# A bucketed attention with a bilinear MLP behind it, on one core: the first two chunks' products by weight group, late weight conversions, bfloat16 scale products and a new order

## The chip, the core and the metric

The kernel runs on one core of a Trainium2 chip. TensorE is written PE, its weight load PEld, VectorE DVE, ScalarE ACT, GpSimd POOL, and SyncE, which here issues all DMAs, SP. The metric is the time of one execution on the device in microseconds (us); lower is better.

## What is computed

Four batches of eight heads, 768 positions, 64 values each. Queries and keys get a bucket of six signs from a projection; a query attends only to keys of its own bucket. The heads' outputs, side by side, are the rows x of a bilinear MLP.

```python
mask = q_bucket[:, :, :, None] == k_bucket[:, :, None, :]
scores = np.where(mask, scale * np.matmul(q, k.transpose(0, 1, 3, 2)), -1000000000.0)
scores = scores - np.max(scores, axis=-1, keepdims=True)
attn = np.exp(scores)
attn = attn / (np.sum(attn, axis=-1, keepdims=True) + 1e-09)
x = np.matmul(attn, v)            # (4, 8, 768, 64), then (3072, 512)
out = ((x @ w_a) * (x @ w_b)) @ w_out      # 512 -> 1536 -> 512
```

## The kernel before

All products run on 16-bit numbers in two parts: each operand is scaled by a power of two and split into a high part and a remainder (`hi`, `lo`), and three of the four partial products are added in PSUM.

**Chunks and query tiles.** The 3072 rows are 12 chunks of 256 (four batches, `NCH` = 3 chunks each). A chunk has two halves of four heads, and each half eight *query tiles* of 128 queries of one head: 192 in all. A query tile (`qtile`, L984) is a chain over all engines. PE makes 128 x 768 scores in PSUM (L1004, four products, tile `s`); DVE takes their maximum `mx` (L1016) and the width (L1025); ACT or DVE makes the bias, ACT the exponentials `e` with their sum (L1048); DVE, ACT or POOL casts them to 16 bits (L1056 to L1058) and POOL or DVE subtracts the cast to get the remainder (L1068, L1072), both into `a2`; SP issues a DMA that turns `a2` into `at` (L1078); PE multiplies it by V (L1087, 18 products, `av`). There are two PSUM tiles `s`, three tiles `e`, four `a2` and three `at`.

**The MLP of a chunk** (`moe`, L1261) has 12 blocks of 128 of the 1536 columns. For each, PE makes a and b (L1285, 24 products into `ab`), ACT copies a with its scale (L1299), DVE multiplies (L1307, `g`), ACT or DVE casts g, POOL subtracts (L1327), and PE adds the block's part of the output (L1337, six products into `o`). Chunk 0 closes `o` after every four blocks, since each of the three groups of weights has a scale of its own (`per_q`, `whole`); the other chunks close it once, with one scale for all (`one_scale`).

**Weights.** w_a and w_b come in three groups of 512 columns each, w_out in three groups of 512 rows: nine conversions (`w_group`, `wo_group`). A group's 64-bit words (`words`, L519) land in four staging tiles or in the places of w_out; DVE takes maxima (L617), PE spreads them over partitions by two fp32 passes with `ident` (L572), a chain of one-column operations on DVE makes the scales, ACT works on the words in place (L540, L548), DVE joins them to fp32 (L555), ACT casts and POOL subtracts (`hi_lo`, L633, L638). K, Q and V of each batch are scaled in the same way (`scale_of`, L450 to L470), K for each pair of heads, and K and Q are turned, so that d lies on partitions, together with their bucket marks in one tile `marked` (`turn`, `buckets`). In batch 0 all four K pairs and the first Q are turned by PE (L834) and copied out of PSUM (L842, L844); all others by DMA (L823).

**What sets the order.** Every operation is recorded with a number, and the table `ORDER` lists the numbers in the order in which they are issued; each engine runs its own in that order. A number of 10000 or more takes another engine for the operation; a negative one issues that many filler products of PE into the unused `ab` (`fill`, L1439, tile `warm`). The keys in the constants (`K0`, `V0`, `WG0`, `MF0` ...) only document where the table comes from; no order is computed from them here.

## Time and profile before

| | |
|---|---|
| median of 3 runs | 922.95 us (919.64 to 923.08) |
| span of the profiled execution, first to last instruction | 918.4 us |
| PE busy | 864.2 us, 94% |
| DVE, ACT, POOL busy | 681.2 us (74%), 543.9 us (59%), 433.0 us (47%) |
| granted PE clock, mean | 0.996 of 2.4 GHz |
| moved by DMA | 147.4 MB in 435950 packets |

The profiled execution's own time is its span and what lies around it: the runs lie 1.2 to 4.7 us above the span. Busy shares are means over a start, in which tiles are prepared and weights converted, and a long stretch in which chunks follow each other; so the windows (busy time of each engine in a stretch) say more than the page's first line. PE's busy time is modelled from pipelined products, so a price of a product is better read as the distance between two starts.

### The profile page before, as it was taken

To read this page: it belongs to the slowest core of one execution; us is meant where nothing else is said; L and a number is where in the kernel's file an instruction comes from. 1 tells how busy PE (TensorE), PEld (TensorE's weight loads), DVE (VectorE), ACT (ScalarE), POOL (GpSimd) and SP (SyncE) were. 2 spreads that over 40 slices of the span, in tenths; PEclk is the share of its full clock that TensorE was granted. 3 is DMA by queue.
4 is the path that set the end of the run, shared out by engine and by line. 5 is a ranking of instruction groups with operands and counts; after the bars stand their busy time and mean duration, and the time that the engine had idled before them with its cause. 6 is when DMAs were issued, how large, how long until landed. Compare 5 with 4: busy or idle time off the path is not lost.

```text
span 918.4 us, 23592 instructions
## 1 busy us (share of the span) xinstructions
PE 864.2 (94%) x9429; PEld 658.4 (72%) x9429; DVE 681.2 (74%) x1622; ACT 543.9 (59%) x1034; POOL 433.0 (47%) x372
## 2 busy tenths in 40 slices
PE   5667789999999999999999999999999999999998
...
DVE  7999999998988778777976757776888863752311
...
GB/s 330 222 238 235 191 224 229 163 189 194 175 193 184 144 144 197 185 172 153 176 110 187 107 141 163 151 208 151 154 187 169 156 126 113 130 111 70 1 24 24
DMA packets 435950, 147.40 MB, mean 161 GB/s; under 512 B 407552, under 2 KB 428160, under 8 KB 435840
## 3 DMA queue, kind: packets, MB, share of 16 engines
...
## 4 chain that ended last, share of the span: by engine, by line
PE 73%; DVE 9%; ACT 1%; issue 1%; DMA 1%; SPq 0%; ACTq 0%; DVEq 0%
PE ab L1285 36%; PE o L1337 18%; PE s L1004 10%; PE av L1087 8%; DVE mx L1016 2%; DVE xz L1187 1%; DVE g L1307 1%; DMA at<-a 1%; SPq L823 0%; PE b_k L795 0%; PE b_q L795 0%; DVE x L1126 0%; DVE width L1025 0%; DVE vl L781 0%; PE ps_v L450 0%
## 5 line engine op out<-in xcount | busy, mean ns | idle before, releaser
L1285 PE MATMUL ab<-xT,wab 128*128 128x256 f16 x3456 | 408.2, 273 | 3.0 <-DVE g L1307 1.8
L1285 PEld LDWEIGHTS <-wab 128*128 128x128 f16 x3456 | 333.1, 98 | 56.3 <-issue 4.1
L1068 POOL TENSOR_TENSOR a<-e,a 128x768 f16<-128x768 f32 x137 | 230.5, 1686 | 132.6 <-ACT a L1057 71.8
L1048 ACT ACTIVATE e<-s,bias,width 128x768 f32<-128x768 f32 x192 | 189.9, 989 | 83.2 <-DVE bias L1038 67.2
L1327 POOL TENSOR_TENSOR g<-g,g 128x256 f16<-128x256 f32 x144 | 106.2, 738 | 235.0 <-ACT g L1315 144.0
L1337 PE MATMUL o<-wo,g 128*128 128x512 f16 x864 | 209.3, 379 | 0.4 <-DVE ob L1373 0.4
L1016 DVE TENSOR_REDUCE mx<-s 128x1 f32<-128x768 f32 x192 | 181.6, 949 | 26.6 <-PE s L1004 25.8
L1307 DVE SCALAR_TENSOR_TENSOR g<-ab,wlow,a 128x256 f32<-128x256 f32 x132 | 63.6, 482 | 139.8 <-ACT a L1299 127.4
L1299 ACT ACTIVATE a<-ab,wlow 128x256 f32<-128x256 f32 x132 | 62.1, 471 | 162.8 <-PE ab L1285 161.4
L1087 PEld LDWEIGHTS <-at 128*128 128x128 f16 x3456 | 123.0, 98 | 25.3 <-DMA at<-a 5.6
L1337 PEld LDWEIGHTS <-g 128*128 128x128 f16 x864 | 81.9, 98 | 74.8 <-issue 0.6
L1087 PE MATMUL av<-vh,at 128*128 128x64 f16 x2304 | 126.4, 193 | 5.2 <-DMA at<-a 3.8
L1004 PE MATMUL s<-kTA_k,qTA_q 128*128 128x384 f16 x384 | 93.7, 326 | 18.2 <-ACT e L1048 13.9
L1004 PE MATMUL s<-kTB_k,qTB_q 128*128 128x384 f16 x384 | 93.7, 326 | 0.0
L1058 POOL CAST a<-e 128x768 f16<-128x768 f32 x57 | 51.1, 896 | 64.6 <-ACT e L1048 56.4
L1057 ACT CAST a<-e 128x768 f16<-128x768 f32 x92 | 76.0, 830 | 1.9 <-DMA at<-a 0.4
L1087 PE MATMUL av<-vl,at 128*128 128x64 f16 x1152 | 65.2, 193 | 0.0
L1315 ACT CAST g<-g 128x256 f16<-128x256 f32 x99 | 39.7, 401 | 38.2 <-DVE g L1307 33.0
L1004 PEld LDWEIGHTS <-qTA_q 128*128 128x128 f16 x384 | 34.7, 98 | 38.2 <-issue 20.8
L1032 ACT ACTIVATE bias<-mx,width 128x1 f32<-128x1 f32 x91 | 26.4, 292 | 57.1 <-DVE width L1025 56.9
L1072 DVE TENSOR_TENSOR a<-e,a 128x768 f16<-128x768 f32 x55 | 55.0, 1000 | 4.3 <-ACT a L1057 3.9
L1004 PEld LDWEIGHTS <-qTB_q 128*128 128x128 f16 x384 | 37.5, 98 | 24.9
...
## 6 DMA issues: line engine op xcount, KB each, us to landing
...
at<-a SPq DMA_TRANSPOSE x192, 4.1
```

What stands on the lines that cost most here:

```text
L1004: nc.tensor.matmul(ps.t[:, jj, :HALF], lhsT=x.t[:, uq, :], rhs=y.t[:, h * NT + jj * 3 : h * NT + jj * 3 + 3, :].rearrange("p t x -> p (t x)"),
L1016: lambda: nc.vector.tensor_reduce(out=mx.t[:, u : u + 1], in_=halves(ps.t), axis=AX.XY, op=ALU.max, negate=True),
L1048: lambda: nc.scalar.activation(flat2(e.t), halves(ps.t), AF.Exp, bias=bias.t[:, u : u + 1], scale=width.t[:, u : u + 1], accum_out=sm.t[:, ...
L1057: ("ACT", 0.725, lambda: nc.scalar.copy(out=a2.t[:, 0], in_=e.t), False),
L1068: lambda: nc.gpsimd.tensor_tensor(out=a2.t[:, 1], in0=e.t, in1=a2.t[:, 0], op=ALU.subtract),
L1072: lambda: nc.vector.tensor_tensor(out=a2.t[:, 1], in0=e.t, in1=a2.t[:, 0], op=ALU.subtract), True,
L1087: nc.tensor.matmul(av.t[:, u, :], lhsT=at.t[:, a + kt, :], rhs=w.t[:, h, kt, :], start=i == 0, stop=i == 3 * NT - 1,)
L1285: nc.tensor.matmul(pl.t[:, m, :CH], lhsT=wt(m, wi, cc, f), rhs=xt.t[:, :, xi * NC + cc, :], start=i == 0, stop=i == 3 * NC - 1,)
L1299: lambda a=a, pl=pl, gr=gr: nc.scalar.activation(a.t, pl.t[:, 0, :CH], AF.Copy, scale=cuts[:, gr : gr + 1]),
L1307: lambda a=a, g32=g32, pl=pl, gr=gr: nc.vector.scalar_tensor_tensor(out=g32.t, in0=pl.t[:, 1, :CH], scalar=cuts[:, gr + 1 : gr + 2], in1=a ...
L1327: lambda g=g, g32=g32: nc.gpsimd.tensor_tensor(out=g[1].t, in0=g32.t, in1=g[0].t, op=ALU.subtract),
L1337: nc.tensor.matmul(po.t[:, u, :], lhsT=g[gi].t[:, us], rhs=wo[f // 2].t[:, f % 2, wi * DM : (wi + 1) * DM], start=f % per_q == 0 and i == ...
```

## The change

The change has five parts.

- **Products by weight group in two chunks.** `SPLIT` = 2: chunks 0 and 1 run their blocks in the order group 0 of chunk 0, group 0 of chunk 1, group 1 of chunk 0, and so on, and close `o` after each group; chunk 1 closes it three times where it closed once.
- **Conversions later.** Only group 0 is converted ahead of its use; groups 1 and 2 are loaded and converted between the products of the groups before them. In group 0 and 1, w_a and w_b share one chain of scales.
- **Words in free slots.** The staging tiles `stg`, `W1`, `W2` (later w_out's places), still unused slots of `wab` and `raw` tiles take the words. Some conversions work on half a tile.
- **Scales by bfloat16 products.** `spread` multiplies the upper 16 bits of a maximum by a bfloat16 identity: one pass in place of two. Batch 0 has one chain for the scales of all four V pairs.
- **A new order**, without fillers, in which K pairs 1 to 3 of batch 0 are turned by DMA (`K_BY_PE` = 1).

```diff
-NE, NA, NAT, NRAW = 3, 4, 3, 2
-POOL_CASTS, POOL_EVERY = 20.26, 4
+NE, NA, NAT, NRAW = 3, 4, 3, 3
+K_BY_PE = 1
+SPLIT = 2
+POOL_CASTS, POOL_EVERY = 0, 4
 ORDER = [
-    12, 6, 5, 52, 0, 2, 1, 40, 3, 13, 60, 4, 296, 53, 14, 295, 7, 299, 15, -1, 8, 16, 300, 10017, 273, 41, 19, 277, 9,
...
+    HOMES = [
+        [("W1", "W2"), (20, 16), ("stg", 10)], [(18, "W2"), ("W1", "stg"), ("W2", 18)],
+        [("W2", "stg"), ("W2", "stg"), ("stg", "raw")],
+    ]
+    def spread(mx, cols, out):
+        for i, c in enumerate(cols):
+            nc.tensor.matmul(
+                out[:, i * P : (i + 1) * P],
+                lhsT=mx.t[:, c : c + 1].bitcast(BF16)[:, 1:2].to_broadcast([P, P]), rhs=identb, start=True, stop=True,
+            )
+    def largest(out, ps, n):
+        nc.vector.tensor_reduce(
+            out=out, in_=ps[:, : n * P].rearrange("p (n x) -> p n x", n=n), axis=AX.X, op=ALU.max
+        )
...
-            lambda: nc.tensor.matmul(
-                ps.t[:, 0, :P], lhsT=mx.t[:, 0:1].to_broadcast([P, P]), rhs=ident, start=True, stop=True
-            ),
+        op("PE", 0.06 * n, lambda: spread(mx, range(n), flat()), key, r=["identb", *((mx, i) for i in range(n))], w=[ps])
...
+    def words(src, home, name, key):
+        if home == "raw":
+            pieces = [buf("raw", [P, WP, 2], I32, f"raw_{name}{i}", NRAW) for i in range(2)]
+        elif isinstance(home, int):
+            pieces = [Slots(home, f"raw_{name}")]
+        else:
+            pieces = [buf(home, [P, 2 * WP, 2], I32, f"raw_{name}", 1, cp)]
...
-    HOME_K0 = [("wo0", 1, cp), ("wo1", 1, cp), ("raw", NRAW, p2), ("raw", NRAW, p2)]
-    HOME_V0 = [("a2", NA, p2)] * 2 + [("at", NAT, p2)] * 2
+    HOME_K0 = [("W0", 1, cp), ("e", NE, p2), ("e", NE, p2), ("e", NE, p2)]
+    HOME_V0 = [("a2", NA, p2)] * 4
...
-        turn(B, 2 * NT, tB, key, [(B, "hi"), (B, "lo")], n, None if b else TURN[0])
+        pe = b == 0 and hp < K_BY_PE
+        turn(B, 2 * NT, tB, key, [(B, "hi"), (B, "lo")], n, TURN[0] if pe else None)
...
-        whole = b or c
+        whole = b * NCH + c >= SPLIT
-        for f in range(NF):
+        for f in range(fqs[0] * (WP // P), (fqs[-1] + 1) * (WP // P)):
...
-                for g in range(NG):
-                    w_group(g, WG0[g], WC0[2 * g : 2 * g + 2], WH0[2 * g : 2 * g + 2])
                 for fq in range(NFQ):
-                    wo_group(fq, WO0[fq], OC0[2 * fq : 2 * fq + 2], OH0[2 * fq : 2 * fq + 2])
+                    for ms in ([0, 1],) if fq < 2 else ([0], [1]):
+                        w_groups(fq, ms, WG0[fq], WC0[fq], WH0[fq])
+                    wo_group(fq, WO0[fq], [OC0[fq]] * 2, [OH0[fq]] * 2)
...
+                elif m == SPLIT - 1:
+                    for fq in range(NFQ):
+                        for x in range(SPLIT):
+                            moe(b, x, [fq], [MF0[SPLIT * fq + x]] * NFQ, pace, lag, False)
```

Three places show what the new order moves. The first is DVE at the first query tiles. Before, behind the fourth score maximum (a row `mx` names batch, chunk and half; the `s` it reads ends with pair, head and tile):

```order
L1016 TENSOR_REDUCE mx_0_0_0_422<-s_0_0_0_0_1_1_538 128x1
L883 SCALAR_TENSOR_TENSOR nB_k0_3_516<-rk_k0_3_83,ks_k0_3_555,nB_k0_3_516 128x12x64
L617 TENSOR_REDUCE wmx_w3_503<-raw_w3_1_424 128x1
L1025 TENSOR_SCALAR width_0_0_0_457<-mx_0_0_0_422,qsig_q0_0_454 128x1
L1038 TENSOR_SCALAR bias_0_0_0_463<-mx_0_0_0_422,width_0_0_0_457 128x1
L973 TENSOR_SCALAR qsig_q0_0_454<-kinv_70,qmx_q0_0_152 128x1 x2
L626 TENSOR_REDUCE wmx_w3_503<-wmx_w3_503 128x1
L617 TENSOR_REDUCE wmx_wo0_511<-raw_wo0_0_206 128x1
L617 TENSOR_REDUCE wmx_wo0_511<-raw_wo0_1_507 128x1 x2
L578 TENSOR_REDUCE al_w3_695<-ps_w3_668 128x1
L626 TENSOR_REDUCE wmx_wo0_511<-wmx_wo0_511 128x1
```

And in the change, from the same maximum to the next two:

```order
L1077 TENSOR_REDUCE mx_0_0_0_377<-s_0_0_0_0_1_1_432 128x1
L1086 TENSOR_SCALAR width_0_0_0_399<-mx_0_0_0_377,qsig_q0_0_296 128x1
L1013 TENSOR_SCALAR qmx_q0_1_440<-qmx_q0_1_440 128x1
L1016 TENSOR_SCALAR qmx_q0_1_440<-qmx_q0_1_440 128x1
L1020 RECIPROCAL qsc_q0_1_453<-qmx_q0_1_440 128x1
L659 TENSOR_REDUCE wmx_w0ab_243<-raw_w0ab_0_0_268 128x1
L659 TENSOR_REDUCE wmx_w0ab_243<-wab_78 128x1
L1077 TENSOR_REDUCE mx_0_0_0_377<-s_0_0_0_1_0_0_466 128x1
L1077 TENSOR_REDUCE mx_0_0_0_377<-s_0_0_0_1_0_1_471 128x1
```

Before, 28 rows stand between the fourth maximum and the fifth, most of them scales and weight rows; now six do.

The second place is SP's queue at the first turns of attention (`at`). Before:

```order
L1078 DMA_TRANSPOSE at_0_0_0_0_0_532<-a_0_0_0_0_0_0_505 128x12x128
L1078 DMA_TRANSPOSE at_0_0_0_0_1_575<-a_0_0_0_0_0_1_529 128x12x128
L927 DMA rq_q_1_84<-in_q_dram 128x8x128
L519 DMA raw_w_0_585<-in_moe_w_a_dram 128x1024 x2
L519 DMA raw_w_1_626<-in_moe_w_a_dram 128x1024 x2
L1078 DMA_TRANSPOSE at_0_0_0_1_0_693<-a_0_0_0_0_1_0_610 128x12x128
L1078 DMA_TRANSPOSE at_0_0_0_1_1_746<-a_0_0_0_0_1_1_691 128x12x128
L823 DMA_TRANSPOSE qTB_q_1_820<-nB_q_1_711 128x16x128
L519 DMA raw_w_1_882<-in_moe_w_b_dram 128x1024 x2
L519 DMA raw_w_0_922<-in_moe_w_b_dram 128x1024 x2
```

In the change:

```order
L883 DMA_TRANSPOSE kTB_k_1_329<-nB_k_1_165 128x12x128
L563 DMA wab<-in_moe_w_b_dram 128x1024
L563 DMA raw_wo_0_0_360<-in_moe_w_out_dram 128x1024
L988 DMA rq_q_1_90<-in_q_dram 128x8x128
L883 DMA_TRANSPOSE kTB_k_2_402<-nB_k_2_350 128x12x128
L883 DMA_TRANSPOSE kTA_k_1_428<-marked 128x12x128
L1139 DMA_TRANSPOSE at_0_0_0_0_0_443<-a_0_0_0_0_0_0_416 128x12x128
L769 DMA rk_k_3_88<-in_k_dram 128x2x384
L563 DMA raw_wo_0_0_360<-in_moe_w_out_dram 128x1024
L1139 DMA_TRANSPOSE at_0_0_0_0_1_461<-a_0_0_0_0_0_1_425 128x12x128
L1139 DMA_TRANSPOSE at_0_0_0_1_0_478<-a_0_0_0_0_1_0_458 128x12x128
```

Turns of K now stand between the loads and the turns of attention, and fewer weight loads do.

The third is POOL, whose remainders `g1` carry batch, chunk and block in their names. Before, at blocks 6 to 9 of chunk 0:

```order
L1327 TENSOR_TENSOR g1_0_0_6_2708<-g_0_0_6_2594,g0_0_0_6_2603 128x256
L638 TENSOR_TENSOR wo4_2735<-wo_y4_2648,wo4_2735 128x2x512
L1327 TENSOR_TENSOR g1_0_0_7_2791<-g_0_0_7_2743,g0_0_0_7_2748 128x256
L1068 TENSOR_TENSOR a2_0_2_0_1_0_0_2767<-e_0_2_0_1_0_0_2751,a2_0_2_0_1_0_0_2767 128x768
L1068 TENSOR_TENSOR a2_0_2_0_1_0_1_2847<-e_0_2_0_1_0_1_2789,a2_0_2_0_1_0_1_2847 128x768
L1068 TENSOR_TENSOR a2_0_2_0_1_1_0_2904<-e_0_2_0_1_1_0_2853,a2_0_2_0_1_1_0_2904 128x768
L1327 TENSOR_TENSOR g1_0_0_8_2968<-g_0_0_8_2860,g0_0_0_8_2888 128x256
L1068 TENSOR_TENSOR a2_0_2_0_1_1_1_2991<-e_0_2_0_1_1_1_2966,a2_0_2_0_1_1_1_2991 128x768
L1327 TENSOR_TENSOR g1_0_0_9_3053<-g_0_0_9_3000,g0_0_0_9_3027 128x256
```

In the change, at the same query tiles of chunk 2:

```order
L1129 TENSOR_TENSOR a2_0_2_0_1_1_0_2104<-e_0_2_0_1_1_0_2097,a2_0_2_0_1_1_0_2104 128x768
L1393 TENSOR_TENSOR g1_0_0_3_2203<-g_0_0_3_2045,g0_0_0_3_2099 128x256
L1129 TENSOR_TENSOR a2_0_2_0_1_1_1_2233<-e_0_2_0_1_1_1_2128,a2_0_2_0_1_1_1_2233 128x768
L1119 CAST a2_0_2_1_0_0_1_2297<-e_0_2_1_0_0_1_2295 128x768
L1129 TENSOR_TENSOR a2_0_2_1_0_0_0_2259<-e_0_2_1_0_0_0_2200,a2_0_2_1_0_0_0_2259 128x768
L683 TENSOR_TENSOR wab_78<-wab_78 128x2x512
L1129 TENSOR_TENSOR a2_0_2_1_0_0_1_2297<-e_0_2_1_0_0_1_2295,a2_0_2_1_0_0_1_2297 128x768
L1393 TENSOR_TENSOR g1_0_1_0_2440<-g_0_1_0_2410,g0_0_1_0_2433 128x256
L1129 TENSOR_TENSOR a2_0_2_1_0_1_0_2399<-e_0_2_1_0_1_0_2340,a2_0_2_1_0_1_0_2399 128x768
L683 TENSOR_TENSOR wab_78<-wab_78 128x2x512
L1393 TENSOR_TENSOR g1_0_1_1_2512<-g_0_1_1_2484,g0_0_1_1_2486 128x256
```

Block 0 of chunk 1 now follows block 3 of chunk 0, attention stands further ahead of the products than before, and weights of a later group are converted between them.

## Rows read from the trace of the kernel before

**Rows 1.** The page: busy time by engine, then busy tenths in 40 slices.

```profile
PE 864.2 (94%) x9429; PEld 658.4 (72%) x9429; DVE 681.2 (74%) x1622; ACT 543.9 (59%) x1034; POOL 433.0 (47%) x372
...
PE   5667789999999999999999999999999999999998
...
DVE  7999999998988778777976757776888863752311
```

**Rows 2.** Windows: stretch and length (us), busy us by engine, clock, DMA share, GB/s.

```profile
0.00:198.50 198.50, 150.83 (x1758) 115.33 (x1759) 185.19 (x448) 166.98 (x253) 113.39 (x79) 0.98 0.97 225
0.00:20.00 20.00, 10.68 (x91) 8.62 (x92) 14.62 (x41) 10.41 (x10) 3.09 (x7) 1.00 0.90 320
20.00:100.00 80.00, 55.64 (x635) 42.52 (x634) 77.18 (x195) 76.03 (x104) 42.88 (x26) 0.96 0.95 237
40.00:160.00 120.00, 93.25 (x1139) 71.94 (x1139) 114.21 (x268) 105.89 (x161) 80.29 (x52) 0.97 1.04 222
200.00:300.00 100.00, 99.83 (x1126) 76.45 (x1124) 86.24 (x211) 55.56 (x113) 50.06 (x44) 1.00 1.01 188
200.00:918.40 718.40, 711.85 (x7662) 541.92 (x7659) 494.46 (x1173) 375.68 (x780) 318.42 (x293) 1.00 0.77 142
```

**Rows 3.** Timeline of DVE (start us, us, what) at the eleventh product g.

```profile
198.53 0.47 DVE L1307 SCALAR_TENSOR_TENSOR g<-ab,wcut,a 128x256 f32<-128x256 f32 x1
```

**Rows 4.** Groups by line of PE: count | busy us, mean ns | idle before.

```profile
L1441 PE MATMUL warm<-ident 128*128 128x256 f16 x273 | 40.4, 287 | 2.2 <-DMA ident<-in_cst_w_dram 2.2
L450 PE MATMUL ps_v<-ident,mx_v 128*128 128x128 f32 x32 | 7.2, 309 | 0.5 <-ACT kTA_k L842 0.5
```

**Rows 5.** The same view of DVE.

```profile
L1016 DVE TENSOR_REDUCE mx<-s 128x1 f32<-128x768 f32 x192 | 181.6, 949 | 26.6 <-PE s L1004 25.8
L1072 DVE TENSOR_TENSOR a<-e,a 128x768 f16<-128x768 f32 x55 | 55.0, 1000 | 4.3 <-ACT a L1057 3.9
L617 DVE TENSOR_REDUCE wmx_w<-raw_w 128x1 f32<-128x512 f32 x24 | 15.9, 676 | 0.0
L555 DVE SCALAR_TENSOR_TENSOR wab<-raw_w 128x1024 int32<-128x1024 int32 x11 | 13.3, 1221 | 0.0
```

**Rows 6.** The same view of ACT.

```profile
L1048 ACT ACTIVATE e<-s,bias,width 128x768 f32<-128x768 f32 x192 | 189.9, 989 | 83.2 <-DVE bias L1038 67.2 <-DVE r L1121 2.4 <-POOL a L1068 2.3
L1057 ACT CAST a<-e 128x768 f16<-128x768 f32 x92 | 76.0, 830 | 1.9 <-DMA at<-a 0.4
L540 ACT ACTIVATE raw_w<-raw_w,wsc 128x1024 f32<-128x1024 f32 x12 | 14.4, 1240 | 0.2 <-DVE wsc L587 0.2
L842 ACT COPY kTA_k<-t_k_ACT 128x1536 f16<-128x1536 f16 x4 | 5.7, 1430 | 0.9 <-PE t_k_ACT L834 0.9
```

**Rows 7.** Timeline of PE where it is full: starts of consecutive groups.

```profile
505.17 1.46 PE L1337 MATMUL o<-wo,g 128*128 128x512 f16 x6
506.47 0.49 PE L1004 MATMUL s<-kTA_k,qTA_q 128*128 128x384 f16 x2
...
507.12 0.34 PE L1087 MATMUL av<-vh,at 128*128 128x64 f16 x6
...
508.17 2.79 PE L1285 MATMUL ab<-xT,wab 128*128 128x256 f16 x24
510.79 0.34 PE L1087 MATMUL av<-vh,at 128*128 128x64 f16 x6
```

**Rows 8.** Turns of attention: their line; a window with little else; SP's timeline there.

```profile
L1078 SPq DMA_TRANSPOSE at<-a x192: 1272/1484/4358, 36.9 to 840.0; - x192
DMA to landing us min/median/max: 3.6/4.1/7.7
96.00:118.00 22.00, 16.02 (x225) 11.96 (x224) 21.05 (x51) 15.80 (x30) 15.60 (x13) 1.00 1.11 199
93.94 23.95 SPq L1078 DMA_TRANSPOSE at<-a  x11
```

**Rows 9.** Windows (columns as in rows 2): PE's granted clock dips.

```profile
80.00:85.00 5.00, 3.38 (x33) 2.45 (x31) 5.00 (x8) 4.97 (x10) 3.91 (x2) 0.71 0.91 298
```

More of the change, by code (lines that the diff above doesn't have):

```diff
@@ L306, in __init__ @@
         self.turn = None
-        if tag in IN_TURN:
+        if tag in IN_TURN and not name.startswith("ps_"):
             self.turn = plan.turns.get((pool, tag), 0)
@@ L470, in rest @@
-            nc.vector.reciprocal(out=sc if inv is None else sc.t, in_=to)
-        op("DVE", 0.48, rest, key, r=[al], w=[al, pw, inv_tok] + ([] if inv is None else [sc]))
+            nc.vector.tensor_scalar(out=al, in0=al, scalar1=low, scalar2=1.0 / top, op0=ALU.max, op1=ALU.mult)
+            nc.vector.reciprocal(out=to, in_=al)
+            nc.vector.tensor_copy(out=sc, in_=to)
+            if inv is not None:
+                nc.vector.tensor_copy(out=inv, in_=al)
+            if eps is not None:
+                nc.vector.tensor_scalar(out=eps, in0=to, scalar1=ESC * 1e-9, scalar2=None, op0=ALU.mult)
@@ new lines, in words, with to_f32, hi, low @@
+        return out
+    def to_f32(halves_, key, dst, dst_toks, scale, rtoks=()):
+        pieces = {}
+        for i, (raw, at) in enumerate(halves_):
+            pieces.setdefault(id(raw), (raw, []))[1].append(i)
+        for raw, parts in pieces.values():
+            n = WP * len(parts)
+            rt = [(raw, "raw", i) for i in parts]
+            dt = [dst_toks[i] for i in parts] if len(dst_toks) > 1 else dst_toks
+            def hi(raw=raw, n=n):
+                return raw.t[:, :n, 1]
+            def low(raw=raw, n=n):
+                return raw.t[:, :n, 0]
+            def to(at=parts[0] * WP, n=n):
+                return dst()[:, at : at + n]
+            op(
+                "ACT", 0.1 + 0.5 * len(parts),
+                lambda hi=hi: nc.scalar.activation(
+                    hi().bitcast(F32), hi().bitcast(F32), AF.Prelu, scale=scale(), alpha=-float(2.0**32)
+                ),
+                key, r=[*rt, *rtoks], w=[(raw, "hi")],
+            )
+            op(
+                "ACT", 0.1 + 0.45 * len(parts),
+                lambda raw=raw, n=n, low=low: nc.scalar.activation(
+                    low(), raw.t[:, :n].bitcast(U8)[:, :, 3], AF.Copy, scale=1.0 / 32, bias=-15.5 / 32
+                ),
+                key, r=rt, w=[(raw, "lo")],
+            )
+            op(
+                "DVE", 0.1 + 0.55 * len(parts),
+                lambda hi=hi, low=low, to=to: nc.vector.scalar_tensor_tensor(
+                    out=to().bitcast(I32), in0=hi(), scalar=3, in1=low(),
+                    op0=ALU.logical_shift_left, op1=ALU.bitwise_or,
+                ),
+                key, r=[(raw, "hi"), (raw, "lo"), *getattr(raw, "toks", ())], w=dt, sbuf=True,
+            )
@@ L584, in power, with scale @@
             nc.vector.tensor_scalar(
-                out=i, in0=al.t.bitcast(I32), scalar1=mask, scalar2=None, op0=ALU.bitwise_and
+                out=out.bitcast(I32), in0=i, scalar1=float(-field << 20), scalar2=float(times), op0=ALU.add, op1=ALU.mult
             )
+        def scale():
+            largest(column(0), flat(), n)
             nc.vector.tensor_scalar(
-                out=i, in0=i, scalar1=float(-field << 20), scalar2=float(times), op0=ALU.add, op1=ALU.mult
+                out=column(0), in0=column(0), scalar1=float(2.0**-14), scalar2=None, op0=ALU.max
@@ L589, in power @@
             )
-        def rest():
-            nc.vector.tensor_scalar(out=al.t, in0=al.t, scalar1=float(2.0**-14), scalar2=None, op0=ALU.max)
-            power(sc.t, 0x7F800000, -1, 143 * 8)
-        op("DVE", 0.46, rest, key, r=[al], w=[(al, "max"), sc])
+            power(sc.t[:, :n], 0x7F800000, -1, 143 * 8)
+        op("DVE", 0.6 + 0.13 * n, scale, key, r=[ps], w=[(ps, "max"), sc])
         def powers():
```

406 lines of the change are left out of this document (205 added, 201 removed), and 385 rows, old and new, of the table ORDER.

## The prediction

> **What bounds the kernel now.** I read the page first, then windows by stage, then the waits and the order of each engine. The page says PE: 94% busy, and from the sixth slice on full in nearly every one [rows 1]. The windows show what that average hides. From 200 us to the end PE is busy 711.9 of 718.4 us, while DVE has 494 and ACT 376: there the time is PE's own work. In the first 198.5 us PE is busy 150.8, and much of that is no work of the program: the 273 filler products (warm) all lie there, 40.4 us of PE [rows 2, 4]. So some 88 us are lost before PE is full (198.5 less 150.8, plus 40.4), and almost nothing after. What fills that first stretch is DVE: 77.2 of 80 us between 20 and 100, 114.2 of 120 between 40 and 160, with ACT just behind (76.0 and 105.9) and the DMA engines at a share near 1 [rows 2]. The kernel is a ramp whose length DVE sets, and then 720 us of PE. What the change is worth is read from the ramp.
>
> I fix one place in the program as the end of the ramp. Before, it is the eleventh product g of DVE (chunk 0, block 10), which starts at 198.53 us [rows 3]; from there on PE is full, and 918.4 - 198.5 = 719.9 us remain. Up to it PE's order holds 45 groups of scores, 39 of attention times V, 12 of a and b, 10 of the second product. In the new order I take the tenth product (chunk 0, block 5), where PE has done nearly as much: 52, 47, 10.5 and 9. Of all products up to the end of chunk 2 it gives the latest end by the count that follows.
>
> **PE after that place.** Unit prices are distances of starts where PE is full [rows 7]: scores 507.12 - 506.47 = 0.65 us, attention times V (508.17 - 507.12)/2 = 0.53, a and b 510.79 - 508.17 = 2.62, the second product 506.47 - 505.17 = 1.30. The new order has 7 x 0.65 + 8 x 0.53 - 1.5 x 2.62 - 1 x 1.30 = 3.6 us more behind it. The scale products become one bfloat16 pass in place of two fp32 ones of 0.31 us each, which overlap [rows 4]. 23 of the old stand after the place; a new one has no row, so the gain is between 0 and 23 x 2 x 0.31 = 14 us; the passes overlap by more than half, so I take 4. **New end = place + 719.9 - 3.6 - 4 = place + 712.3.** The fillers, the fewer turned blocks (56 in place of 128) and the early scale products are in front of the place and count only there.
>
> **DVE up to the place.** Counted from the two orders, with mean durations, those of the larger in [rows 5]: 8 fewer maxima of weight rows (36 to 28) x 0.676 = -5.4; 7 fewer joins of words (18 to 11) x 1.22 = -8.5; 42 fewer one-column operations (scales by group, one chain for four V pairs) -8.3; 4 fewer subtractions x 1.0 = -4.0; fewer splits of weights, q maxima and others -12; against it 9 more score maxima (43 to 52) x 0.949 = +8.5, 15 more widths and biases +3.2, K and V maxima, bucket marks and the rest +6.5. Sum -20 of 204, which stand for 185.2 busy us [rows 2]; so 18 us less busy, and with DVE as full as before the place comes at **180**.
>
> **ACT up to the place.** Here nothing is saved: 9 more exponentials x 0.99 = +8.9 and 8 more casts x 0.83 = +6.6, more K and q splits and maxima +9, against 9 fewer word passes x 1.24 = -11.2, 5 fewer copies of turned blocks x 1.43 = -7.2, 7 fewer weight casts -7.3 [rows 6]. So still 166 of the 167 busy us. ACT does 10.4 of them in the first 20 us [rows 2]. At its fullest, 0.95 from 20 to 100, the rest takes 164 us and the place is at 184; at its mean of 40 to 160, 0.88, it is at **197**. ACT, off the path before, is now as tight as DVE.
>
> **DMA and SP up to the place.** The old stretch moved 225 GB/s x 198.5 = 44.7 MB. The new order has 8 more turns of attention and 10 of K (pairs 1 to 3 and the next batch now by DMA), each 128 x 1536 values of 2 bytes, 0.39 MB, so +7.1; two more K or V loads +0.8; 7 fewer weight loads of 0.52 MB, -3.7; one smaller turn of x, -0.3: 48.6 MB. At 190 us that is 256 GB/s; the first 20 us ran at 320, 20 to 100 at 237 [rows 2]. On SP's queue the 18 turns cost an issue of 1.48 us each, 27 us, against 7 loads. K's turns also hold the one tile `marked` for their landing, 4.1 us in the median [rows 8] instead of PE's fraction of that, and behind POOL's next copy into it stand its casts and subtractions; POOL, 113 of 198.5 us busy, has the room.
>
> **Edits with no price.** Six closings of o in place of four for the first two chunks add four additions on DVE; PE has a and b meanwhile. Words staged in free slots remove waits of SP for a conversion (SP's loads stood behind it) and cost nothing on an engine. After the place the late conversions, some 20 us of DVE and 12 of ACT, meet a DVE that was 86.2 of 100 us busy from 200 to 300 [rows 2]; that is full, not over, and the count at the later products stays below the place's.
>
> **Sum.** DVE says 180, ACT 184 to 197. In the old stretch 20 to 100 both were over 95% full at once [rows 2], so two full engines need not cost much; three with DMA will cost some. I take **189**: 189 + 712.3 = 901.3 of span. The median of the runs, 922.95, is 4.5 above the profiled span, so **906**.
>
> **Rivals.**
> - **DVE alone, the others follow** (180): 892 + 4.5 = 897. For it: the old order's DVE was 96% full beside a busy ACT. Against: ACT's 166 us.
> - **The DMA engines become the bound; slower.** Place: the turns of attention in chunks 0 and 1, which share SP's queue with K's turns and the weight loads. If 48.6 MB move at the 237 GB/s of 20 to 100, the place is at 205; at the 225 of the whole stretch, 216; ends 922 to 933. For it: the share was already 0.95 to 1.04 [rows 2]. Against: at 1.11 for 22 us [rows 8] eleven turns went out in 24 us, and a share counts packets that overlap. It decides from the point where a turn lands later than about 7 us: three tiles `at` and 3.1 us a query tile (52 in some 162 us) leave 9.3 us for a landing and PE's reading.
> - **Without fillers PE runs at half clock.** Even with them the granted clock was 0.71 in 80 to 85 us, one of its two levels (1.2 GHz) for part of it [rows 9]; PE had been waiting between groups. Before the ramp's end PE has slack, so half clock costs through the chain alone: scores and V products of one tile take 1.18 us more, and with three tiles in flight 0.4 us a tile; over 40 tiles 16 us: 922. The Trainium skill (TensorE: Matmul & The Clock Gate, section "HAM oscillation — how this bites in real kernels") says that a PE which waits between bursts drops back to half clock and pays for the way up each time; it speaks for this rival and against dropping fillers, and by it the sum would be 922 and not 906. The trace agrees that dips occur, not that they are long.
>
> **How the numbers follow.** Forecast 906 (place 184 to 197: 901 to 914) 0.55; DVE alone, 897, 0.15; DMA 0.2; clock 0.1. A measurement here tells 0.5%, 4.6 us, from no change: faster is below 918.3, slower above 927.6. Faster: nearly all of the first two, a fifth of the others: 0.73. Same: the lower half of the DMA case and most of the clock's, 0.15. Slower: the upper half of the DMA case and what I have not seen, 0.12. Range 891 to 929: down past the second case by the unknown gain of the scale products, up into the third.
>
> **What would show it.** Right: the tenth product near 189 us; DVE and ACT both over 0.9 busy from 20 on; PE over 0.98 busy from about 190; no warm group; landing of attention's turns near 5 us. Wrong by DMA: landing medians over 7 us, SP waiting for PE's reads of `at`, DVE below 0.9. Wrong by the clock: granted clock well under 1 past 60 us. Wrong altogether: a hole in PE after 200 us, waiting for the weights of groups 1 or 2.

## The result: 1.1% slower

The changed kernel takes 932.05 us (median of 4 runs, 930.24 to 935.07) against 921.63 us of the kernel before on the same chip: ratio 1.0114, 95% interval 1.0085 to 1.0143. The profiled execution has a span of 933.0 us; 906 us was forecast, with a span of 901.3; 929 was the upper end of the range.

Below, "place" is what the prediction calls so: the eleventh product g of DVE in the kernel before and its variants, the tenth in the changed kernel and its variants. To set runs of different chips against the change, the difference of two ratios is taken; 0.01 is 9.2 us, and with such intervals some 3 us is the least that can be told apart. A place is read from one profiled execution each; the change's (935.07 us) was the slowest of its four, so a place that moves by less than some 3 us is not read as a gain.

### The profile page after: what moved, and what is told of

It reads as the page before. It is cut to its first block, busy times and chain, and to the rows that moved or that the text cites. A ratio compares the mean times of both kernels' runs of the same rounds, so it can differ in the third digit from the quotient of the medians.

```text
span 933.0 us, 22762 instructions
## 1 busy us (share of the span) xinstructions
PE 848.7 (91%) x9042; PEld 632.3 (68%) x9042; DVE 665.3 (71%) x1576; ACT 542.3 (58%) x1039; POOL 445.2 (48%) x384
## 4 chain that ended last, share of the span: by engine, by line
PE 50%; DVE 17%; DMA 8%; issue 5%; ACT 5%; POOL 3%; SPq 1%; ACTq 0%; DVEq 0%; POOLq 0%
PE ab L1351 25%; PE o L1403 12%; PE s L1065 7%; PE av L1148 5%; DVE mx L1077 4%; DMA at<-a 4%; ACT e L1109 2%; DMA vr<-in_v_dram 2%; DVE g L1373 2%; POOL a L1129 2%; DVE a L1133 1%; ACT a L1118 1%; DMA rk_k<-in_k_dram 1%; DVE xz L1248 1%; DVE nB_k L943 1%
## 5 line engine op out<-in xcount | busy, mean ns | idle before, releaser
L1129 POOL TENSOR_TENSOR a<-e,a 128x768 f16<-128x768 f32 x145 | 242.5, 1676 | 122.7 <-ACT a L1118 61.3
L1148 PEld LDWEIGHTS <-at 128*128 128x128 f16 x3456 | 128.7, 101 | 45.1 <-DMA at<-a 24.4
L1148 PE MATMUL av<-vh,at 128*128 128x64 f16 x2304 | 131.3, 197 | 20.0 <-DMA at<-a 18.9
L1373 DVE SCALAR_TENSOR_TENSOR g<-ab,wlow,a 128x256 f32<-128x256 f32 x120 | 57.7, 481 | 109.9 <-ACT a L1365 101.7
L1365 ACT ACTIVATE a<-ab,wlow 128x256 f32<-128x256 f32 x120 | 56.4, 470 | 123.1 <-PE ab L1351 117.2
L1065 PE MATMUL s<-kTA_k,qTA_q 128*128 128x384 f16 x384 | 101.0, 347 | 23.7 <-ACT e L1109 15.1
L1065 PE MATMUL s<-kTB_k,qTB_q 128*128 128x384 f16 x384 | 101.4, 348 | 0.0
L1118 ACT CAST a<-e 128x768 f16<-128x768 f32 x97 | 80.0, 828 | 6.5 <-DMA at<-a 5.1
L1119 POOL CAST a<-e 128x768 f16<-128x768 f32 x55 | 47.3, 860 | 71.5 <-ACT e L1109 67.0
L1133 DVE TENSOR_TENSOR a<-e,a 128x768 f16<-128x768 f32 x47 | 50.3, 1073 | 3.5 <-ACT a L1118 3.2
```

The costliest lines, as they stand in the source:

```text
L1065: nc.tensor.matmul(ps.t[:, jj, :HALF], lhsT=x.t[:, uq, :], rhs=y.t[:, h * NT + jj * 3 : h * NT + jj * 3 + 3, :].rearrange("p t x -> p (t x)"),
L1118: ("ACT", 0.725, lambda: nc.scalar.copy(out=a2.t[:, 0], in_=e.t), False),
L1129: lambda: nc.gpsimd.tensor_tensor(out=a2.t[:, 1], in0=e.t, in1=a2.t[:, 0], op=ALU.subtract),
L1133: lambda: nc.vector.tensor_tensor(out=a2.t[:, 1], in0=e.t, in1=a2.t[:, 0], op=ALU.subtract), True,
L1148: nc.tensor.matmul(av.t[:, u, :], lhsT=at.t[:, a + kt, :], rhs=w.t[:, h, kt, :], start=i == 0, stop=i == 3 * NT - 1,)
L1365: lambda a=a, pl=pl, gr=gr: nc.scalar.activation(a.t, pl.t[:, 0, :CH], AF.Copy, scale=cuts[:, gr : gr + 1]),
```

## The profile after

The page of the changed kernel: busy times, the 40 slices, and what DMA moved.

```profile
PE 848.7 (91%) x9042; PEld 632.3 (68%) x9042; DVE 665.3 (71%) x1576; ACT 542.3 (58%) x1039; POOL 445.2 (48%) x384
...
PE   2656696989999999999999999999999999999998
...
DVE  7888889879887868877866756876877964752311
...
PEclk9956799899999999999999999999999999999999
...
DMA packets 445353, 149.69 MB, mean 160 GB/s; under 512 B 416960, under 2 KB 437568, under 8 KB 445248
```

Against [rows 1] PE is less busy (the fillers are gone), DVE's first slices are no longer nines, and the clock line has a valley from 47 to 117 us. Windows of the changed kernel, with the columns of [rows 2]:

```profile
0.00:208.50 208.50, 140.82 (x1531) 97.79 (x1532) 174.73 (x411) 166.82 (x273) 123.99 (x91) 0.84 1.06 234
20.00:100.00 80.00, 48.48 (x479) 30.58 (x477) 68.77 (x147) 66.04 (x103) 46.43 (x32) 0.72 1.05 227
40.00:160.00 120.00, 82.60 (x976) 56.90 (x974) 104.27 (x238) 100.45 (x170) 81.76 (x55) 0.77 1.10 228
200.00:300.00 100.00, 95.48 (x987) 71.79 (x988) 84.03 (x196) 64.73 (x114) 56.94 (x47) 0.98 0.84 178
208.50:933.00 724.50, 707.88 (x7513) 534.55 (x7510) 490.53 (x1166) 375.48 (x767) 321.17 (x294) 1.00 0.70 139
```

And DVE's timeline at the tenth product, the answer to [rows 3]:

```profile
208.51 0.48 DVE L1373 SCALAR_TENSOR_TENSOR g<-ab,wcut,a 128x256 f32<-128x256 f32 x1
```

The place is at 208.5 us, not at 189; 724.5 us follow it, not 712.3. Two misses, then: 19.5 us before the place and 12.2 behind it. Before it no engine is full any more: DVE is busy 68.8 of 80 us where it was 77.2, ACT 66.0 where it was 76.0. What is nearly full is the feed of the turns. SP's timeline of the changed kernel from 60 to 100 us:

```profile
58.93 3.17 SPq L883 DMA_TRANSPOSE qTA_q<-marked  x1
62.16 1.50 SPq L883 DMA_TRANSPOSE kTB_k<-nB_k  x1
63.71 0.89 SPq L563 DMA_DIRECT2D raw_w1ab<-in_moe_w_b_dram  x1
64.64 0.44 SPq L563 DMA_DIRECT2D raw_wo<-in_moe_w_out_dram  x1
65.26 1.27 SPq L1139 DMA_TRANSPOSE at<-a  x1
67.27 3.83 SPq L883 DMA_TRANSPOSE kTA_k<-marked  x1
71.26 1.40 SPq L1139 DMA_TRANSPOSE at<-a  x1
72.70 0.58 SPq L563 DMA_DIRECT2D raw_w1ab<-in_moe_w_b_dram  x1
73.40 8.21 SPq L1139 DMA_TRANSPOSE at<-a  x3
81.74 0.99 SPq L563 DMA_DIRECT2D raw_w1ab<-in_moe_w_a_dram  x2
83.32 5.22 SPq L1139 DMA_TRANSPOSE at<-a  x2
88.59 0.57 SPq L988 DMA_DIRECT2D rq_q<-in_q_dram  x1
89.28 7.62 SPq L1139 DMA_TRANSPOSE at<-a  x3
96.95 0.57 SPq L563 DMA_DIRECT2D wab<-in_moe_w_a_dram  x1
98.01 1.66 SPq L1139 DMA_TRANSPOSE at<-a  x1
```

There is hardly a gap: issues alone take 35.8 of these 40 us, where in the kernel before they take 30.0. A row with x3 holds three turns and what lies between them; one turn holds the queue for 1.27 to 5.09 us. All of SP's rows up to the place, summed by kind, in both traces (a wait that a DMA's own row carries is no row, so the waits are a lower bound):

| up to the place | before (198.5 us) | changed (208.5 us) |
|---|---|---|
| turns issued, us on the queue | 49, 103.2 (2.11 each) | 66, 138.0 (2.09 each) |
| loads issued, us | 54, 27.8 | 49, 27.7 |
| turns and loads alone, us | 131.0, 66% | 165.7, 79% |
| rows of waits for a semaphore, us | 23.9 | 18.8 |
| queue taken, with these waits | 154.9, 78% | 184.5, 88% |

The theory this gives: **SP's queue and the DMA engines behind it now hold the start** (called SPQ where the queue's time is meant, RATE where the bytes are). Its rivals: CLOCK (PE at half clock without fillers), ORDER (PE meets V products before their turn has landed and the scores stand behind them), and COUPLED (everything waits on everything).

## The experiments

### PE's clock: e1, e2, e3

e1 puts 304 fillers into the gaps that PE has between 8 and 118 us, e2 440; each call of `fill` takes a fresh tile. The first rows of e1:

```diff
-    13, 7, 5, 6, 3, 75, 2, 77, 27, 79, 1, 14, 4, 15, 81, 63, 257, 261, 16, 17, 18, 258, 76, 297, 78, 10028, 29, 20,
-    80, 19, 21, 30, 8, 9, 10022, 82, 83, 10, 31, 11, 32, 84, 64, 12, 23, 87, 65, 259, 66, 24, 262, 265, 91, 68, 39,
+    13, 7, 5, 6, 3, 75, 2, 77, 27, 79, 1, 14, 4, 15, 81, 63, 257, 261, 16, 17, 18, 258, 76, 297, 78, 10028, -36, 29, 20,
+    80, 19, 21, 30, 8, 9, 10022, 82, 83, 10, 31, 11, 32, 84, 64, 12, -18, 23, 87, 65, 259, 66, 24, 262, 265, 91, 68, 39,
...
```

> The change with 304 filler products of 128 x 256 (0.107 us each at full clock, 32.5 us in all) put back into the gaps that PE has between 8 and 118 us, 70% of each gap. Theory CLOCK (PE at half clock for 65 of the 165 us between 40 and 205 us stretches every score and V product on the chain of a query tile): the granted clock is over 0.95 from 60 to 119 us, the tenth product g comes 10 to 20 us earlier (189 to 199 us instead of 208.5) and the time is 912 to 924 us. Theory DMA (48.9 MB must land before that product, at some 230 GB/s): the clock rises all the same, but the tenth product stays at 205 to 210 us and the time at 928 to 935 us.

> As the run before, but 440 fillers, which fill each of those gaps wholly at full clock. CLOCK: the clock is as full as with 304; a filler that overruns a gap delays a score product that is waited for, so the time is the same as with 304 or up to 5 us longer. DMA: 928 to 937 us.

e3 takes all negative numbers out of the table of the kernel before.

```diff
-    12, 6, 5, 52, 0, 2, 1, 40, 3, 13, 60, 4, 296, 53, 14, 295, 7, 299, 15, -1, 8, 16, 300, 10017, 273, 41, 19, 277, 9,
+    12, 6, 5, 52, 0, 2, 1, 40, 3, 13, 60, 4, 296, 53, 14, 295, 7, 299, 15, 8, 16, 300, 10017, 273, 41, 19, 277, 9,
...
```

> The kernel before without its 273 fillers and nothing else. CLOCK: the mean granted clock falls from 0.996 to 0.95 to 0.98 and the time rises by 8 to 20 us, to 930 to 942 us. DMA, or DVE alone as the bound of the start: the clock falls, the time stays within 3 us of 921.6.

Measured: e1 943.74 us (ratio 1.0246, 1.0227 to 1.0266), e2 944.75 us (1.0263, 1.0239 to 1.0287), e3 920.51 us (0.9997, 0.9982 to 1.0011). The window 60 to 100 us (columns of [rows 2]) of the changed kernel, of e1, of e3 and of the kernel before:

```profile
60.00:100.00 40.00, 24.67 (x260) 16.00 (x259) 33.07 (x62) 30.70 (x51) 24.73 (x16) 0.64 1.10 226
```

```profile
60.00:100.00 40.00, 28.20 (x354) 20.48 (x353) 32.94 (x62) 31.35 (x52) 23.54 (x14) 0.95 1.14 224
```

```profile
60.00:100.00 40.00, 21.94 (x201) 13.50 (x199) 38.47 (x86) 36.66 (x56) 26.98 (x14) 0.65 0.98 230
```

```profile
60.00:100.00 40.00, 29.62 (x327) 21.64 (x328) 38.96 (x92) 38.53 (x60) 27.04 (x15) 0.96 1.03 234
```

Fillers bring the clock from 0.64 to 0.95, and in these 40 us DVE and ACT do not a microsecond more work for it: that the clock holds the start is not borne out. The clean half is e3: the old kernel runs as long at 0.65 as it does with fillers at 0.96. In the changed kernel the test is not clean, since the fillers cost time of their own, which could hide a gain of the clock. The Trainium skill (TensorE: Matmul & The Clock Gate, section "HAM oscillation — how this bites in real kernels") says that a PE which waits between bursts falls back and pays; the trace agrees on the fall, and e3 shows no price where PE is not what the others wait for. That the fillers cost 12 us in the changed kernel (1.0246 against 1.0114) was not expected: e1 and e2 lie above the ranges of both theories. e2's more fillers cost no more that can be told apart; the place is at 216.4 us in e1 and a turn holds SP 2.25 us on average. At the twenty-first score maximum, 96.7 us in e1 and 97.0 in the change, nothing is lost yet. What makes the loss behind it was not found.

### Where the turns and their issues stand: e4 to e8

e4 leaves K's six turns of batch 0 out.

```diff
+        if b == 0 and hp >= 1:
+            tA, tB = kT[b, hp] = kT[b, 0]
...
+        if shared:
+            op("SP", 0.0, lambda: None, key, r=[*toks, dst])
+            return
```

> The change with the six DMA turns of K pairs 1 to 3 of batch 0 left out: these pairs read the turned tiles of pair 0, so the scores of six heads of batch 0 are computed from the wrong keys. It takes 2.4 MB and six issues on SP's queue out of the first 90 us. DMA: the tenth product comes 8 to 12 us earlier and the time is 919 to 925 us. CLOCK: the places where PE waits for a turned K (9.5 us in all) close, but the clock stays at half there; 926 to 933 us.

927.13 us, ratio 1.0068 (1.0046 to 1.0089), some 4 us faster than the change; the place at 200.9 us, 7.6 earlier. SP is taken for 162.5 us up to there. This falls just short of what the feed theories gave (8 to 12 us at the place, 919 to 925 us) and lies in the range of CLOCK, 926 to 933; and as e4 also closes the places where PE waited for a turned K, its gain can't be put down to the feed alone. The place's 7.6 us are from the profiled executions, the 4 us from the medians, and the change was profiled in its slowest.

e5 turns the same K pairs by PE, e6 issues all weight loads on POOL's queue.

```diff
+        if evict == "both":
+            ps = psum(f"t_{name}", "o")
...
+                nc.scalar.copy(out=dst.t.rearrange("p u x -> p (u x)"), in_=o[:, : n * P])
```

```diff
-                lambda i=i, raw=raw, at=at: nc.sync.dma_start(
+                lambda i=i, raw=raw, at=at: nc.gpsimd.dma_start(
```

> The change with K pairs 1 to 3 of batch 0 turned by PE again (twelve products of 128 and one ACT copy of 1.43 us for each of the six turns), at the places where SP issued the DMAs. Theory SPQ (SP's queue is what holds the start: 184.5 of the 208.5 us before the tenth product are issues and waits on it, a turn 2.1 us): six turns at 2.64 us, 16 us, leave the queue; with 8.6 us more on ACT the tenth product comes 4 to 9 us earlier, 923 to 928 us. Theory RATE (the DMA engines' rate, 48.9 MB before that product at 235 GB/s): 2.4 MB less, the same 923 to 928. Theory ORDER (PE meets the V products before their turn has landed, 16.1 us, and the scores stand behind them): no gain, 929 to 935.

> The change with the 24 weight loads issued on POOL's queue instead of SP's, at the same places of the order; not a byte less is moved. SPQ: some 19 of them at 0.57 us, 11 us, leave SP's queue before the tenth product, which comes 4 to 9 us earlier; 923 to 928 us. RATE: same bytes, 929 to 935. POOL, busy 69% from 60 to 120 us, may lose by it: a load that waits for its place stands in front of casts and subtractions there; if that is what happens, slower than 935 with POOL's waits longer.

e5: 947.36 us (1.0280, 1.0247 to 1.0314). e6: 953.02 us (1.0358, 1.0285 to 1.0431). e5 missed on the slow side; e6 went beyond the 935 us of its third case, but not by longer waits of POOL (for ACT's casts 20.8 us up to 210 us, where the change has 23.5). Much of the loss is made at once: the third score maximum, at 34.5 us in the change, comes at 42.3 in e5 and 42.1 in e6. From the fifth maximum to the place e5 takes 170 us, the change 169: the relief of 2.4 MB and six turns, as much as in e4, gained nothing behind the late start. That speaks against a feed that holds the start alone.

What holds the first scores is in ACT's timelines, of the changed kernel, of e6 and of e5:

```profile
14.52 1.04 ACT L998 ACTIVATE nB_q<-rq_q 128x1024 bf16<-128x1024 f32 x1
```

```profile
22.46 1.06 ACT L998 ACTIVATE nB_q<-rq_q 128x1024 bf16<-128x1024 f32 x1 [4.11 <-DMA rq_q<-in_q_dram]
```

```profile
38.01 1.44 ACT L887 COPY kTB_k<-t_k 128x1536 f16<-128x1536 f16 x1 [4.10 <-PE t_k L886]
```

In e6 the first Q lands at 22.4 us, in the change at 13.3: eight weight loads that POOL issued from 4.4 us on landed ahead of it. In e5 a copy of a turned K stands in ACT's order before the first exponential, which starts at 39.7 us and not at 31.7. So the late starts come from where the edits put these operations, and the two runs do not tell SPQ from RATE.

e7 moves six V products (and one operation of DVE that reads them) behind the next scores, e8 has four tiles `at`.

```diff
-    218, 10219, 310, 205, 212, 225, 220, 331, 226, 320, 221, 321, 227, 213, 10228, 229, 169, 188, 234, 461, 235,
+    218, 10219, 310, 205, 212, 225, 220, 331, 226, 320, 221, 321, 227, 213, 10228, 229, 169, 234, 188, 461, 235,
...
```

```diff
-NE, NA, NAT, NRAW = 3, 4, 3, 3
+NE, NA, NAT, NRAW = 3, 4, 4, 3
```

> The change with six V products (of 1.06 to 3.36 us of idle PE before them, 10.1 us in all, waiting for the turn) put one score product later in the order. ORDER: the scores no longer stand behind a turn; the tenth product comes 5 to 9 us earlier and the time is 922 to 927 us. SPQ and RATE: the turns land no earlier and the wait only moves; 929 to 934 us.

> The change with four tiles `at` instead of three. Before the tenth product SP waits 9.8 us for PE's reads of `at` (seven times). SPQ: these waits go, the tenth product comes 2 to 6 us earlier, 926 to 931 us. RATE: the turns are issued earlier and take longer to land; 930 to 935 us. ORDER: part of PE's waits go, 926 to 931.

e7: 935.32 us (1.0139, 1.0112 to 1.0166), place 207.5. e8: 932.33 us (1.0103, 1.0072 to 1.0135), place 206.9. Neither can be told from the change: for the six products moved ORDER falls, and three tiles `at` are not what holds the turns. In e8 the rows of SP's waits fell from 18.8 to 11.3 us and nothing came of it: the range of RATE (930 to 935 us), not that of SPQ (926 to 931).

### One dose of work for each engine: e9 to e13, e15, e16

If one resource holds the start, work added there comes out at the end, and work added elsewhere does not. Each run adds operations that nobody reads, spread from 44 to 196 us. The body for SP; for the others it is a subtraction on DVE, a copy on ACT or POOL, or a load of 0.39 MB:

```diff
+    junk = cp.tile([P, P, NBITS], F32, tag="junk", name="junk")
...
+            nc.sync.dma_start(out=junk[:D, 0, :], in_=proj)
```

> The change with 16 further subtractions of 128 x 768 on DVE, written to a tile nobody reads, spread evenly over the order from 44 to 196 us: about 1.0 us each, 16 us. If DVE holds the start (as it did before): 14 to 18 us slower than the change, 946 to 950 us. If another engine or queue does: under 5 us slower. Theory COUPLED (no engine is full, but every queue is in a fixed order and stands behind the others through two tiles s, three e, three at, so that a delay on any of them moves all): 5 to 13 us slower, and the same for ACT, POOL and SP.

> The change with 19 further copies of 128 x 768 on ACT, spread in the same way: about 0.83 us each, 16 us. If ACT holds the start: 14 to 18 us slower than the change (946 to 950 us). If another does: under 5 us. COUPLED: 5 to 13 us.

> The change with 19 further copies of 128 x 768 on POOL, spread in the same way: about 0.86 us each, 16 us. If POOL holds the start (subtractions of 1.68 us between the cast and the turn): 14 to 18 us slower than the change (946 to 950 us). If another does: under 5 us. COUPLED: 5 to 13 us.

> The change with 30 further loads of 1.5 KB on SP's queue, spread in the same way: some 0.5 us each on the queue, 15 us, and no bytes to speak of. SPQ: 10 to 16 us slower than the change (942 to 948 us). If the DMA engines' rate holds the start, or DVE, ACT or POOL: under 4 us slower. COUPLED: 4 to 13 us.

> The change with 10 further loads of 0.39 MB (3.9 MB, at 235 GB/s 16.7 us of the DMA engines) on SP's queue, spread from 44 to 196 us; on the queue some 0.6 us each, 6 us. SPQ (the queue's time is what counts; 20 us more of it gave 10.9): 2 to 5 us slower than the change, 934 to 937 us. RATE (the bytes count): 12 to 18 us slower, 944 to 950 us.

> The kernel before with the same 30 further loads of 1.5 KB on SP's queue between 44 and 196 us, some 20 us of the queue as measured in the change. SP's queue there is taken for 154.9 of 198.5 us. If the change moved the bound of the start onto SP's queue: under 5 us slower than before, under 926 us (10.9 us in the change). If SP's queue was the bound before as well: 8 to 15 us slower.

> The kernel before with the same 16 further subtractions on DVE between 44 and 196 us, some 25 us as measured in the change. If DVE holds the start there, as the prediction read it: 18 to 26 us slower than before (939 to 947 us), against 7 us in the change. If not: under 10 us.

What the doses really took, by their own rows, for e9, e12, e15 and e16 (nanoseconds min/median/max):

```profile
L1516 DVE TENSOR_TENSOR junk<-pj x16: 943/1554/2399, 43.5 to 201.1; 128x768 f16<-128x768 f32 x16
```

```profile
L1516 SPq DMA_DIRECT2D junk<-in_proj_dram x30: 466/578/1396, 43.9 to 210.7; - x30
```

```profile
L1440 SPq DMA_DIRECT2D junk<-in_proj_dram x30: 465/486/1347, 45.3 to 200.7; - x30
```

```profile
L1441 DVE TENSOR_TENSOR junk<-pj x16: 941/1082/2886, 48.9 to 221.2; 128x768 f16<-128x768 f32 x16
```

| dose | kernel | us added there (sum of its rows) | time, ratio to before | what came out |
|---|---|---|---|---|
| DVE (e16) | before | 24.3 | 949.28, 1.0306 (1.0283 to 1.0329) | 28 |
| SP queue (e15) | before | 20.2 | 926.04, 1.0063 (1.0046 to 1.0079) | 6 |
| DVE (e9) | changed | 25.7 | 939.21, 1.0189 (1.0160 to 1.0218) | 7 |
| ACT (e10) | changed | 19 x 0.82 = 15.5 | 931.49, 1.0115 (1.0090 to 1.0139) | 0 |
| POOL (e11) | changed | 19 x 0.83 = 15.7 | 932.06, 1.0129 (1.0092 to 1.0166) | 1 |
| SP queue (e12) | changed | 18.8 | 942.88, 1.0239 (1.0211 to 1.0267) | 12 |
| DMA bytes (e13) | changed | 3.9 MB, 16.7 at 235 GB/s; 5.7 of the queue | 943.87, 1.0251 (1.0222 to 1.0280) | 13 |

This is the main evidence. In the kernel before, DVE's dose comes out whole and more, as the prediction read it; SP's comes out by less than a third (e16 lies above its 18 to 26 us, e15 between its two cases, under 5 and 8 to 15). In the changed kernel DVE's dose comes out by a quarter, ACT's and POOL's not at all, and both doses for the feed, queue and bytes, by six tenths and more. (Counted at 1.00 us each [rows 5], DVE's doses are 16 us each; the feed still gives back the larger share of its dose in the changed kernel.) So the bound has moved from DVE to the feed in the main, not wholly: DVE's 7 us lie in the range of COUPLED (5 to 13), and PE was dosed by e1 and e2 alone, whose 42.9 and 55.0 us of fillers came out as 12 and 14. That everything waits on everything falls with ACT and POOL. A dose shows what more of a resource costs; that less of it gains as much is not shown, as e5 says.

Queue and bytes can't be parted: each dose moved one almost without the other, and both came out. The seen link is the turn, which holds the queue while earlier DMAs are in flight: of the 66 turns 41 hold it under 2 us, 1.52 in the mean, and 25 longer, 3.03 in the mean; 1.9 earlier DMAs had not landed when a short one started, 2.6 when a long one did. The DMA share is 1.08 from 20 us to the place. No run tests this link by itself.

### Loads on ACT's queue: e14

```diff
-                lambda i=i, raw=raw, at=at: nc.sync.dma_start(
+                lambda i=i, raw=raw, at=at: (nc.sync if "0" in name.split("_")[0] else nc.scalar).dma_start(
```

> The change with the weight loads of groups 1 and 2 issued on ACT's queue, where 19 further copies cost nothing, instead of SP's; the same bytes at the same places of the order. SPQ: some 7 us leave SP's queue before the tenth product, which comes 3 to 6 us earlier; 926 to 930 us. RATE: 930 to 934 us.

945.99 us (1.0272, 1.0230 to 1.0314), 15 us slower than the change, place 225.0: a miss for both theories. The loads hold ACT for only 0.33 to 0.72 us each, but SP, rid of 17 loads up to the place, was taken no less: a turn of attention held it 2.32 us where it had held it 1.94. In the profiled execution most of the loss is one hole: the twelfth score maximum comes at 78.2 us, in the change at 65.4. SP and DVE there, in e14:

```profile
59.88 9.71 SPq L883 DMA_TRANSPOSE qTA_q<-marked  x1
```

```profile
77.89 0.36 DVE L938 COPY marked<-nB_k 128x768 f16<-128x768 f16 x1 [11.08 <-DMA qTA_q<-marked]
```

This turn of Q landed 18.0 us after its issue began, with loads of ACT's queue in flight; from 72 to 78 us DMA moved 61 to 130 GB/s at a share over 1.1. This execution was the slowest of e14's four (949.51 us); the fastest, 941.01 us, still lies 10 us above the change. Why this turn was so slow is open.

The Trainium skill (DMA: Bandwidth & Descriptors, section "Issuing engines are not separate DMA queues") says that DMAs of all issuing engines end on the same DMA engines and that a second issuer saves only the issue time, "which is usually small relative to the DMA itself". With the first half e14 agrees. The second does not hold here: a turn's issue is 2.09 us in the mean, and its landing, counted from the start of the issue, 4.9 in the median (for attention's turns in the changed kernel):

```profile
DMA to landing us min/median/max: 3.2/4.9/8.1
```

### The holes behind the place, and one part alone: e18, e17

Behind the place PE's starts, summed by kind without its gaps, give 707.4 us of work where the kernel before has 712.9; its gaps give 12.0 us where the kernel before has 2.1. What the holes wait for, in PE's waits of the changed kernel from 208.5 to 925 us (us, times, longest):

```profile
PE ab L1351 <- DVE g L1373: 7.0, 8, 1.5
PE av L1148 <- DMA at<-a: 2.8, 4, 1.8
PE s L1065 <- ACT e L1109: 1.4, 4, 0.6
```

Two of those g in DVE's timeline, one behind a join of late weight words, one behind a maximum of K that waits for its load:

```profile
213.38 3.15 DVE L606 SCALAR_TENSOR_TENSOR wab<-raw_w2a 128x1024 int32<-128x1024 int32 x1
216.46 0.47 DVE L1373 SCALAR_TENSOR_TENSOR g<-ab,wcut,a 128x256 f32<-128x256 f32 x1
...
386.96 0.95 DVE L785 TENSOR_REDUCE mx_k<-rk_k 128x1 f32<-128x768 f32 x1 [2.27 <-DMA rk_k<-in_k_dram]
387.83 0.47 DVE L1373 SCALAR_TENSOR_TENSOR g<-ab,wlow,a 128x256 f32<-128x256 f32 x1
```

And PE's timeline at the products that waited for them:

```profile
216.98 1.25 PE L1351 MATMUL ab<-xT,wab 128*128 128x256 f16 x10 [1.24 <-DVE g L1373]
...
388.36 0.81 PE L1351 MATMUL ab<-xT,wab 128*128 128x256 f16 x6 [1.21 <-DVE g L1373]
```

e18 puts seven such operations behind their g; e17 gives the kernel before the bfloat16 scale products and the one copy that makes their identity, nothing else.

```diff
-    377, 1208, 1151, 393, 1156, 405, 699, 970, 11152, 378, 700, 1165, 401, 1157, 394, 705, 406, 402, 973, 701, 1136,
+    377, 1208, 1151, 1156, 405, 699, 970, 11152, 378, 700, 393, 1165, 401, 1157, 394, 705, 406, 402, 973, 701, 1136,
...
```

```diff
-                ps.t[:, 0, :P], lhsT=mx.t[:, 0:1].to_broadcast([P, P]), rhs=ident, start=True, stop=True
+                ps.t[:, 0, :P], lhsT=mx.t[:, 0:1].bitcast(BF16)[:, 1:2].to_broadcast([P, P]), rhs=identb, start=True, stop=True
```

> The change with seven DVE operations that stand in front of a product g put behind it (two joins of weight words of group 2, a maximum of K, a cast, a subtraction, two of V and K preparation): PE waits 1.24, 1.20, 1.21, 0.47, 0.88, 1.53 and 0.27 us for these g, 6.8 us in all. If the holes of PE after 200 us are put right by the order of DVE alone: 4 to 7 us faster than the change, 925 to 928 us. If the holes are only filled to come back later (DVE has no room): 930 to 934 us.

> The kernel before with one part of the change alone: the scale products as one bfloat16 pass in place of two fp32 ones, order and fillers as they were. After the place PE's fp32 passes take 5.4 us there (46 of 0.118 us, by distances of starts), the 22 bfloat16 ones of the change 1.6. If that part is worth what the traces say: 3 to 4.5 us faster than before, 916 to 918 us. If it is worth nothing where PE is full: 919 to 923.

e18: 928.44 us (1.0068, 1.0045 to 1.0091), some 4 us faster than the change; PE's wait for g from 207 to 925 us falls (the same view of e18):

```profile
PE ab L1351 <- DVE g L1373: 2.4, 4, 1.6
```

So DVE's order made the greater part of these waits. That the 4 us come from there is not shown: e18 was profiled in the slowest of its six executions (933.04 us), and there the stretch behind the place takes 723.9 us, only 0.6 less than in the change, with 9.3 us of gaps and 2.1 us more between its other starts. e17: 920.14 us against 921.01, ratio 0.9979 (0.9968 to 0.9991): 0.2% faster than the kernel before, where 916 to 918 us was expected of a part that is worth what the traces say. Behind the place its scale products take 1.3 us where 46 fp32 passes took 5.4, but the place comes at 200.9 us, 2.4 later, which gives back over half.

## Why the prediction was wrong

Span forecast 901.3 + 19.5 (place late) + 9.9 (new holes) + 2.1 (less work saved) + 0.2 (the end) = 933.0. The prediction's last term, 4.5 us from the span to the median, came out as -0.95 (933.0 to 932.05). It was scatter: executions of the kernel before with both on record lie 1.7 to 1.9 us above their own span, so the one profiled for the prediction, with 918.4, was one of the faster.

- **What bounds the kernel before: right.** A ramp that DVE sets: e16 shows it.
- **PE after the place: nearly right.** Work fell by 5.5 us, not 7.6; of this the scale products gave 3.8 (5.4 to 1.6), taken as 4. The reason given for the 4 was not in the rows: by [rows 4] 32 passes of 309 ns take 7.2 us, an overlap of about a quarter and not of over half; by distances of starts a pass costs 0.118 us.
- **DVE, ACT and DMA up to the place: counted nearly right.** DVE 174.7 us busy (counted 167), ACT 166.8 (166), 234 GB/s x 208.5 us = 48.8 MB (48.6).
- **"Sum. DVE says 180, ACT 184 to 197 ... I take 189": this step failed.** It closed the sum with two engines that no longer set the pace: a dose on DVE came out by a quarter, on ACT not at all, on the feed by six tenths and more. SP's queue was priced as a difference, "the 18 turns cost an issue of 1.48 us each, 27 us, against 7 loads", and never laid beside the place as DVE and ACT were. 1.48 is a median, which hides the tail; the mean up to the place in the same trace is 2.11, and in the run 17 more turns took 34.8 us more of the queue while five fewer loads gave back 0.1. At 2.11, 66 turns are 139 us, and 49 loads at 0.51 are 25: 164 us of issues, where the kernel before had 131 and 67.5 us beside them, waits and gaps. A place at 189 left 25 us for that rest. Measured are 165.7 us of issues and 42.8 beside them.
- **The DMA rival had it**, with a chance of 0.2: place 205 to 216, end 922 to 933; measured 208.5 and 932.05. It counted by the rate alone; the runs leave open how much of it is rate and how much queue. Of its signs DVE under 0.9 came (0.86 from 20 to 100). The point from which it should decide, landings over 7 us, was wrong: the median landing up to the place is 4.9 us. A landing is counted from the start of the turn's own issue, so the time that a turn stands behind others on the queue does not show in it. The row held against this rival, eleven turns in 23.95 us [rows 8], holds waits too: the issues are 19.5 us of it.
- **The clock rival had the sign and not the price.** 0.72 from 20 to 100 us, but e3 shows such a clock to cost nothing in the kernel before, and in e1 lifting it brought no gain that could be seen beside the cost of the fillers.
- **"After the place the late conversions ... that is full, not over": failed.** A mean of 84 busy us in 100 says nothing of who stands in front of whom. One tile `ab` lets PE wait for a single g, and "a hole in PE after 200 us" was named only as what would be wrong altogether, with no price.
